# A fused attention and two-layer-pair kernel: low parts by products for unit 0 alone, two chunks loaded to other places, blocks alternating every two units

## The chip, the cores and the metric

The kernel runs on one core of a Trainium2 chip. The metric is the device time of one execution in microseconds. A core has a matrix engine (TensorE, PE in the profile, with its weight loads as PEld), VectorE (DVE), ScalarE (ACT), GpSimd (POOL) and SyncE (SP), which here issues all the transfers. Each engine takes its instructions strictly in program order.

## What is computed

Three stages on fp32 data, each feeding the next:

```python
# 1: decayed linear attention, batch 4, 8 heads, 768 steps, head size 48
state = alpha[:, :, t, :, None] * state + einsum('bhd,bhe->bhde', k[:, :, t], v[:, :, t])
y[:, :, t] = einsum('bhd,bhde->bhe', q[:, :, t], state)
# 2: x is y as 3072 tokens of 384; w_a, w_b 384 x 1536, w_out 1536 x 384
x = (x @ w_a) * (x @ w_b) @ w_out
# 3: w_in 384 x 2048, w_out 2048 x 384
h = x @ w_in
out = (maximum(h, 0) + alpha * minimum(h, 0)) @ w_out
```

The weights arrive as 64-bit floats, in halves that the kernel itself has to put together.

## The kernel before, in words

The 3072 tokens are six blocks of four chunks of 128 tokens. A block's four chunks (one for each batch entry) go through the attention, which leaves the block's x in `xt[n]`; then the block's 512 columns go through stage 2, and at the end all blocks go through stage 3.

**fp32 by three products.** PE multiplies values rounded to its fast format (fp32r). Every operand is therefore split into a high part h and a low part l, and a product is h*h + l*h + h*l (`mm3`, lines 601 to 604). One such product of 128x128 by 512 columns is three matmuls; a step of stage 2 (one half of a unit for one block) is 27 of them: nine into `pa`, nine into `pb`, nine into the three accumulators `acc`.

**Units.** Stage 2's hidden size 1536 is cut into six units of 256. Unit u has three weights, a, b and o, each 128 x 768. Each is loaded raw as 64-bit words and converted by `conv` (from line 224): ScalarE takes the magnitude into a tile c (line 253), DVE takes the sign (256), puts it in (261), keeps the power of two (265) and forms what fp32 leaves over (270), ScalarE rounds to the high part (276). Then comes the low part, x - high + rest. There are two ways: with `on_pe` false, two DVE operations (`sub`, line 279, `low`, line 282); with `on_pe` true, three fp32 products with plus and minus the identity into a PSUM tile `cl` (lines 307 to 309), in two halves of 384 columns, each evacuated by ScalarE (312). `PE_UNITS = 3` sends the nine weights of units 0, 1 and 2 the second way. The weights a0 and b0 are converted in two halves throughout, and are loaded raw to the places of later weights (`w17`, `w16`).

**Segments.** `SEGMENTS` says in which order blocks meet units: (block, first unit, end). Blocks 0 and 1 alternate: block 0 with units 0 to 2, block 1 with units 0 to 2, then both with 3 to 5. After a segment the accumulators go to a partial sum `part`: the first segment of a block is copied by ScalarE (`evict1`), a later one is added by DVE, three operations of 512 columns.

**A chunk of attention** (`chunk(g)`). Loads: ra (decays, line 365), kq (369), v (373; in block 0 also vg). DVE: scan backwards (387), reciprocal (393), scan forwards (397), scale k and q (402). PE: transpose k (`kps`, 440), scores (`A`, 457), state update (`dS`, 481), output (`y`, from 491). DVE masks the two score tiles (`As`, 464). ScalarE and DVE split y into the high (564) and low (568) part of x. Tiles ra, kq and v have two buffers each (`tp`), so chunk 2 waits for chunk 0's; `Ring` objects hold these waits.

**The order of work** is written by a planner. `Graph` collects operations with an engine, an assumed duration, a due key and their dependencies; `run` plays them through as a list schedule and emits each engine's instructions in the order that results. Where it sees PE idle for over 500 ns, `fill` (line 177 and on) emits dummy bf16 products `wp` for seven tenths of the hole, one per 110 ns.

Of the kernel before, what the change touches and what calls it, by code (L numbers as in the profile page):

```python
# [11 lines left out]
F32 = mybir.dt.float32  # L12
# [9 lines left out]
P = 128  # L22
CH = 128
# [1 line left out]
MB = BC * CH  # L25

SEGMENTS = (
    (0, 0, 3), (1, 0, 3), (0, 3, 6), (1, 3, 6),
    (2, 0, 6), (3, 0, 6), (4, 0, 6), (5, 0, 6),
)  # L30
LAG = 2

PE_UNITS = 3


MM = 228
# [102 lines left out]
def body(tc, akq, v, vg, w_a, w_b, w_o1, w_in, w_o2, beta, out):  # L139
# [3 lines left out]
    NU1, NU2 = w_a.shape[0], w_in.shape[0]  # L143
    F1, F2 = 2 * NU1, 2 * NU2
    UC = w_a.shape[2]
    NJ = H // 2
    D = KT * P // H
    GR = 64 - D
    NA = NJ * (CH + 1) + 1
# [3 lines left out]
    with ExitStack() as ctx:  # L153
        ctx.enter_context(tc.manual_schedule())
        pool = lambda name, bufs=1, **k: ctx.enter_context(tc.tile_pool(name=name, bufs=bufs, **k))
        const, wpool, pers = pool("const"), pool("wpool"), pool("pers")
        xpool, cpool, gpool, tp = pool("xpool", 2), pool("cpool", 2), pool("gpool", 2), pool("tp", 2)
# [50 lines left out]
        G = Graph(fill)  # L208
# [3 lines left out]
        flat = [(n, i, s) for s, (n, u0, u1) in enumerate(SEGMENTS) for i in range(2 * u0, 2 * u1)]  # L212
# [10 lines left out]
        def conv(src, tag, name, key, wait, sink, early=15000, on_pe=False, halves=None):  # L223
# [14 lines left out]
            for n in range(2 if halves else 1):  # L238
# [61 lines left out]
                for h in range(2 // N):  # L300
                    cut = lambda x, h=h: x[:, :, h * UC // 2 : (h + 1) * UC // 2] if N == 1 else x
                    p = {}

                    def add(p=p, cut=cut, c1=c1, c2=c2, hi=hi):
                        t = ps_mm.tile([P, MB], F32, name="cl", tag="mm")
                        o = p["t"] = t[:, 0 : UC // 2].rearrange("p (t f) -> p t f", t=nt)
                        nc.tensor.matmul(o, ident, cut(c1()), start=True, stop=False)  # L307
                        nc.tensor.matmul(o, minus, cut(hi()), start=False, stop=False)
                        nc.tensor.matmul(o, ident, cut(c2()), start=False, stop=True)

                    def low_pe(p=p, cut=cut, lo=lo):
                        nc.scalar.copy(cut(lo()), p["t"])
                        sink(b["r"])

                    y = G.add("PE", 900, add, key, [x], pool=mpool)
                    cring.use(y)
                    ev = G.add("ACT", 500, low_pe, key, [y], after=[ev])
                    y.hold.append(ev)
# [3 lines left out]
        def as_unit(r, n):  # L322
            return tuple(y.rearrange("p (t f) -> p t f", t=n) for y in (r[:, 0:UC], r[:, UC : 2 * UC]))

        done, slot_of, taken = {}, {}, {}
        for u in range(NU1):
            for nm, src in (("a", w_a), ("b", w_b), ("o", w_o1)):
                x = nm, u
                slot_of[x] = len(slot_of)
                uses[x] = []  # L330

                def sink(r, x=x):
                    units[x] = as_unit(r, 2 if x[0] == "o" else KT)


                spare = {("a", 0): 3 * NU1 - 1, ("b", 0): 3 * NU1 - 2}.get(x)
                ld, done[x] = conv(src[u], f"w{slot_of[x]}", f"{nm}{u}", due[x] - 20000,
                                   taken.pop(slot_of[x], ()), sink, on_pe=u < PE_UNITS,
                                   halves=None if spare is None else (f"w{spare}", KT))
                if spare is not None:  # L340
                    taken[spare] = done[x]

# [9 lines left out]
        def chunk(g):  # L352
# [6 lines left out]
            def A(eng, dur, fn, deps, early=0, lat=0, after=()):  # L359
                return G.add(eng, dur, fn, key - early, deps, lat, after)  # L360


            def load_a():
                s["ra"] = tp.tile([P, 2 * NA - 1], F32, name="ra", tag="ra")
                nc.sync.dma_start(s["ra"][:, NA - 1 :], akq[g, :, 0:NA])

            def load_kq():
                s["kq"] = tp.tile([P, 2, NJ, CH], F32, name="kq", tag="kq")
                nc.sync.dma_start(s["kq"].rearrange("p s j t -> p (s j t)"), akq[g, :, NA:])

            def load_v():
# [6 lines left out]
            kT = lambda: s["kq"][:, 0]  # L378
            qT = lambda: s["kq"][:, 1]
            r0 = lambda: s["ra"][:, 0 : NA - 1].rearrange("p (j t) -> p j t", j=NJ)[:, :, 0:1]  # L380
            la = A("SP", 800, load_a, rring.take(), 14000, 2500)
            lq = A("SP", 1500, load_kq, lring.take(), 13800, 2500, [la])
            lv = A("SP", 1000, load_v, vring.take(), 12000, 2500)


# [20 lines left out]
            sa = before["scan"] = A("DVE", 1250, scan_a, [rc])  # L406
            slack = SLACK if not start else 0
            k1 = q1 = A("DVE", 1220, mul, [lq, sa], 0, slack)
            rring.use(k1)


            zs = None
            if not start:
                def decayed():
                    z = Z[:, c, :, :]
                    nc.vector.tensor_tensor(out=z, in0=z, in1=r0().to_broadcast([P, NJ, D]),
                                            op=ALU.mult)

                zs = A("DVE", 360, decayed, [r, *state[c]])
                rring.use(zs)  # L420

            def ps_tile(nm, bank=None):
                if start and bank is not None:
# [12 lines left out]
            if not end:  # L436
                def pe_k():
                    s["kps"] = ps_tile("kps", 0)
                    for j in range(NJ):
                        nc.tensor.transpose(s["kps"][:, j, :], kT()[:, j, :], ident)  # L440

                def ev_k():
                    s["ks"] = tp.tile([P, NJ, P], F32, name="ks", tag="ks", bufs=1)
                    nc.scalar.copy(s["ks"], s["kps"])

                w, hold = bank(0)
                x = A("PE", 480, pe_k, [k1, *w])
                ks = A("ACT", 600, ev_k, [x, *kring.take()])
                hold.append(ks)
                lring.use(x)  # L450

            def pe_a():
                s["A"] = [ps_tile(f"A{i}", i + 1) for i in range(2)]
# [21 lines left out]
            if ks is not None:  # L475
                def pe_d():
                    s["dS"] = ps_att.tile([P, NJ, D], F32, name="dS", tag="att")
                    for j in range(NJ):
                        for i in range(2):
                            hs = slice(64 * i, 64 * i + 64)  # L480
                            nc.tensor.matmul(s["dS"][hs, j, :], s["ks"][:, j, hs],
                                             s["v"][:, 2 * j + i, 0:D], start=True, stop=True)

                ds = A("PE", 500, pe_d, [ks, lv, *aring.take()])
                dhold = aring.last()
                kring.use(ds)
                vring.use(ds)
# [29 lines left out]
                for j in range(NJ):  # L517
                    inter(j, j == NJ - 1)

            py = A("PE", 1350 if start else 500 if moved else 1600, pe_y, [a0, a1, lv, q1, zs, *aring.take()])  # L520
            yhold = aring.last()
            if moved:
                def ev_3():
                    s["y3"] = shift[:, KT, :]
                    nc.scalar.copy(s["y3"], s["y"][:, KT, :])

                def pe_m():
                    for j in range(KT):
                        intra(j, j == 0, False)
                    for j in range(KT):  # L530
                        inter(j, False)
                    for j in range(KT):
                        nc.tensor.matmul(s["y"][:, j, :], shift[:, j, :], s["y3"], start=False,
                                         stop=j == KT - 1)

                x = A("ACT", 280, ev_3, [py, *yring.take()])
                py = A("PE", 1900, pe_m, [x])
                yring.use(py)
            lring.use(pa, py)


            if not end:
# [173 lines left out]
        for k, (n, i, s) in enumerate(flat):  # L716
            u, o = divmod(i, 2)
            x = lambda n=n: xt[n]
            b = {}
            pa, ma, ba = up(at[k], [done["a", u][o], *xdone[n]], x, ("a", u), o,  # L720
                            [d for j in range(k - 1) for d in done["o", flat[j][1] // 2]
                             if flat[j][1] // 2 < PE_UNITS and k < 12] + [up_before])
            pb, mb, bb = up(at[k] + 9 * MM, [done["b", u][o], *xdone[n]], x, ("b", u), o, [pa])
            up_before = pb
            xuse[n].extend((pa, pb))

            def copy_a(b=b, ba=ba):
                b["a"] = gpool.tile([P, MB], F32, name="a_sb", tag="a_sb")
                nc.scalar.copy(b["a"], ba["t"])  # L729

            def mul(b=b, bb=bb):
                nc.vector.tensor_tensor(out=b["a"], in0=b["a"], in1=bb["t"], op=ALU.mult)  # L732

            ca = G.add("ACT", 590, copy_a, at[k] - URGENT, [pa, *bring.take()])
            ml = G.add("DVE", 690, mul, at[k] - URGENT, [ca, pb])
            ma.append(ca)
            mb.append(ml)
            glo[k] = gsplit((1, k), at[k] - URGENT, [ml], lambda b=b: b["a"])
            ghold[k] = gring.last()
            bring.use(glo[k])  # L740
            if k >= LAG:
                down1(k - LAG)
# [171 lines left out]
```

## Time and profile before

| | |
|---|---|
| device time, median of 3 runs | 1001.33 us (1000.56 to 1001.47) |
| the profiled execution | 1001.07 us |
| its span, first to last instruction | 999.4 us |
| PE busy | 985.8 us, 99% |
| PE's weight loads busy | 794.2 us, 79% |
| DVE busy | 594.8 us, 60% |
| ACT busy | 256.8 us, 26% |
| read and written in HBM | 74.8 MB and 26.7 MB |

Busy times count an instruction from its start to its end. Matmuls overlap, so a matmul's own duration is longer than the distance to the next one's start; where PE is full, the distance between starts is what an instruction costs. DVE's instructions overlap a little too. Idle time of an engine that is not the bottleneck costs nothing.

### The profile page before, as it was taken

Reading aid. Unit: us, or ns where it says so; the run is one execution under the profiler, and the core shown is the slowest. Engines: PE = TensorE matmul, PEld = TensorE weight load, DVE = VectorE, ACT = ScalarE, POOL = GpSimd, SP = SyncE. Lnnn points to the kernel's source line nnn. Section 1 sums busy time; section 2 is a strip of 40 time slices with the busy share of each in tenths; the row PEclk is TensorE's granted clock in tenths of the full one; section 3 lists DMA queues with packets and bytes.
Section 4 is the critical chain, followed back from the end, with each engine's and each line's share of the span. In section 5 each row is a group of like instructions: output and inputs, shape, how many; then the busy total and the mean of one; then the engine's idle time right before and its main releaser. Section 6 shows DMA issues by size and latency. Waiting matters only on the chain.

```text
span 999.4 us, 12894 instructions
## 1 busy us (share of the span) xinstructions
PE 985.8 (99%) x5364; PEld 794.2 (79%) x5364; DVE 594.8 (60%) x860; ACT 256.8 (26%) x421; POOL 5.5 (1%) x18
## 2 busy tenths in 40 slices
PE   6999999999999999999999999999999999999998
PEld 5776788877888888788778888888888888888886
DVE  7877798258768876884432225554554555545543
ACT  2444443232333333332122112111121111111111
POOL 2000000000000000000000000000000000000000
PEclk9999999999999999999999999999999999999999
DMA  9941200044544744551226561020020100200000
GB/s 364 362 181 53 65 12 11 1 169 117 185 155 152 252 185 147 209 195 55 64 79 221 190 221 64 1 95 1 1 95 1 64 31 1 95 1 1 32 0 32
DMA packets 30922, 103.92 MB, mean 104 GB/s; under 512 B 3472, under 2 KB 3984, under 8 KB 30864
## 3 DMA queue, kind: packets, MB, share of 16 engines
q1 hardware_dynamic: 30864, 103.11, 29.3%
q8 instruction: 42, 0.69, 0.3%
q14 instruction: 16, 0.13, 0.0%
HBM read 74.78 MB, written 26.74 MB: 102 GB/s over the span
## 4 chain that ended last, share of the span: by engine, by line
PE 99%; DVE 0%; DMA 0%; ACT 0%; issue 0%; DVEq 0%; ACTq 0%
PE acc L601 12%; PE acc L604 12%; PE acc L602 12%; PE pi L601 7%; PE pi L602 7%; PE pi L604 7%; PE pb L601 5%; PE pa L601 5%; PE pa L602 5%; PE pa L604 5%; PE pb L602 5%; PE pb L604 5%; PE A L457 3%; PE y L491 2%; PE y L497 2%; PE cl L307 1%
## 5 line engine op out<-in xcount | busy, mean ns | idle before, releaser
L624 ACT CAST gh<-ng 128x512 fp32r<-128x512 f32 x96 | 59.6, 621 | 327.6 <-DVE ng L828 275.0
L824 DVE TENSOR_SCALAR ng<-pi,betaT 128x512 f32<-128x512 f32 x96 | 72.1, 751 | 106.7 <-PE pi L604 105.8
L732 DVE TENSOR_TENSOR a_sb<-a_sb,pb 128x512 f32<-128x512 f32 x72 | 49.5, 687 | 113.8 <-PE pb L604 111.7
L628 DVE TENSOR_TENSOR gl<-ng,gh 128x512 fp32r<-128x512 f32 x96 | 66.4, 691 | 79.8 <-ACT gh L624 79.8
L601 PE MATMUL pi<-x,v 128*128 128x512 f32 x288 | 113.3, 393 | 0.0
L602 PE MATMUL acc<-gh,v 128*128 128x512 f32 x288 | 112.9, 392 | 0.0
L604 PE MATMUL acc<-gl,v 128*128 128x512 f32 x288 | 112.8, 392 | 0.0
L602 PE MATMUL pi<-x,v 128*128 128x512 f32 x288 | 112.7, 391 | 0.0
L601 PE MATMUL acc<-gh,v 128*128 128x512 f32 x288 | 112.4, 390 | 0.0
L601 PE MATMUL pb<-x,wb 128*128 128x512 f32 x216 | 87.0, 403 | 0.0
L601 PE MATMUL pa<-x,wa 128*128 128x512 f32 x216 | 86.3, 399 | 0.0
L601 PE MATMUL acc<-gh,wo 128*128 128x512 f32 x216 | 85.8, 397 | 0.0
L604 PE MATMUL acc<-gl,wo 128*128 128x512 f32 x216 | 84.9, 393 | 0.0
L602 PE MATMUL acc<-gh,wo 128*128 128x512 f32 x216 | 84.7, 392 | 0.0
L602 PE MATMUL pa<-x,wa 128*128 128x512 f32 x216 | 84.6, 392 | 0.0
L602 PE MATMUL pb<-x,wb 128*128 128x512 f32 x216 | 84.6, 391 | 0.0
L604 PE MATMUL pi<-x,v 128*128 128x512 f32 x288 | 81.5, 391 | 0.0
L729 ACT COPY a_sb<-pa 128x512 f32<-128x512 f32 x72 | 42.3, 587 | 151.3 <-PE pa L604 151.3
L624 ACT CAST gh<-a_sb 128x512 fp32r<-128x512 f32 x72 | 44.7, 621 | 132.8 <-DVE a_sb L732 132.8
L828 DVE SCALAR_TENSOR_TENSOR ng<-pi,ng 128x512 f32<-128x512 f32 x96 | 66.4, 691 | 3.1
L601 PEld LDWEIGHTS pi<-x,v 128*128 128x128 f32 x288 | 54.1, 188 | 13.8 <-DVE ng L828 2.1
L601 PEld LDWEIGHTS acc<-gh,v 128*128 128x128 f32 x288 | 54.1, 188 | 12.1
(107 smaller groups left out, 1472.4 us busy)
## 6 DMA issues: line engine op xcount, KB each, us to landing
kq<-in_akq SPq DMA_DIRECT2D x24, 512.0 KB, 3.7
w2d<-ws SPq DMA_DIRECT2D x16, 768.0 KB, 3.4
v<-w2d SPq DMA_DIRECT2D x16, 768.0 KB, 5.5
x2d<-x SPq DMA_DIRECT2D x18, 512.0 KB, 3.4
x<-x2d SPq DMA_DIRECT2D x6, 1536.0 KB, 7.0
ra<-in_akq SPq DMA_DIRECT2D x24, 258.5 KB, 2.8
v<-in_v SPq DMA_DIRECT2D x24, 256.0 KB, 4.3
rs<-in_w_in SPq DMA_DIRECT2D x8, 768.0 KB, 4.6
```

Source lines behind the costliest of these rows:

```text
L457: nc.tensor.matmul(s["A"][i][:, j, :], kT()[ps, j, :], qT()[ps, j, :], start=True, stop=True)
L491: nc.tensor.matmul(s["y"][64 * i : 64 * i + 64, j, :], s["v"][:, 2 * j + i, :], s["As", i][:, j, :], start=first, stop=last)
L497: nc.tensor.matmul(s["y"][ps, j, :], Z[ps, c, j, :], qT()[ps, j, :], start=False, stop=last)
L601: nc.tensor.matmul(o, lh, rh, start=first and n == 0, stop=False)
L602: nc.tensor.matmul(o, ll, rh, start=False, stop=False)
L604: nc.tensor.matmul(o, lh, rl, start=False, stop=last and n == len(pairs) - 1)
L624: nc.scalar.copy(gq[idx][0], src())
L628: nc.vector.tensor_tensor(out=gl, in0=src(), in1=gh.bitcast(F32), op=ALU.subtract)
L729: nc.scalar.copy(b["a"], ba["t"])
L732: nc.vector.tensor_tensor(out=b["a"], in0=b["a"], in1=bb["t"], op=ALU.mult)
L824: nc.vector.tensor_scalar(out=b["n"], in0=bh["t"], scalar1=0.0, scalar2=betaT[:, i : i + 1], op0=ALU.min, op1=ALU.mult)
L828: nc.vector.scalar_tensor_tensor(out=b["n"], in0=bh["t"], scalar=0.0, in1=b["n"], op0=ALU.max, op1=ALU.add)
```

## The change

Three edits, with one set of retuned planner durations.

1. `ON_PE` takes the place of `PE_UNITS`: of the nine weights that form their low part by products into `cl`, a0, b0 and o0 are left. The six weights of units 1 and 2 take the DVE way. The first products of a block no longer wait in the plan for the o weights of such units.
2. Chunks 2 and 3 of block 0 load ra and kq to `w14`, `w15` and `w12`, `w13`, the places of o4, a5, a4 and b4, and not to the two rotating buffers. The loads of those weights wait for the chunks in turn. They leave the rings, so that later chunks wait for others.
3. Blocks 0 and 1 alternate after every two units and not after every three: six segments in place of four.

```diff
@@ -25,12 +25,12 @@
 MB = BC * CH
 
 SEGMENTS = (
-    (0, 0, 3), (1, 0, 3), (0, 3, 6), (1, 3, 6),
+    (0, 0, 2), (1, 0, 2), (0, 2, 4), (1, 2, 4), (0, 4, 6), (1, 4, 6),
     (2, 0, 6), (3, 0, 6), (4, 0, 6), (5, 0, 6),
 )
 LAG = 2
 
-PE_UNITS = 3
+ON_PE = (("a", 0), ("b", 0), ("o", 0))
 
 
 MM = 228
@@ -312,7 +312,7 @@
                         nc.scalar.copy(cut(lo()), p["t"])
                         sink(b["r"])
 
-                    y = G.add("PE", 900, add, key, [x], pool=mpool)
+                    y = G.add("PE", 1600, add, key, [x], pool=mpool)
                     cring.use(y)
                     ev = G.add("ACT", 500, low_pe, key, [y], after=[ev])
                     y.hold.append(ev)
@@ -322,7 +322,7 @@
         def as_unit(r, n):
             return tuple(y.rearrange("p (t f) -> p t f", t=n) for y in (r[:, 0:UC], r[:, UC : 2 * UC]))
 
-        done, slot_of, taken = {}, {}, {}
+        done, slot_of, taken, loads = {}, {}, {}, {}
         for u in range(NU1):
             for nm, src in (("a", w_a), ("b", w_b), ("o", w_o1)):
                 x = nm, u
@@ -335,8 +335,9 @@
 
                 spare = {("a", 0): 3 * NU1 - 1, ("b", 0): 3 * NU1 - 2}.get(x)
                 ld, done[x] = conv(src[u], f"w{slot_of[x]}", f"{nm}{u}", due[x] - 20000,
-                                   taken.pop(slot_of[x], ()), sink, on_pe=u < PE_UNITS,
+                                   taken.pop(slot_of[x], ()), sink, on_pe=x in ON_PE,
                                    halves=None if spare is None else (f"w{spare}", KT))
+                loads[slot_of[x]] = ld
                 if spare is not None:
                     taken[spare] = done[x]
 
@@ -360,12 +361,25 @@
                 return G.add(eng, dur, fn, key - early, deps, lat, after)
 
 
+            spare = 3 * NU1 - 4 - 2 * (c - 2) if start and c >= 2 else None
+            if spare is None:
+                rwait, lwait = rring.take(), lring.take()
+                rhold, lhold = rring.last(), lring.last()
+            else:
+                rwait, lwait, rhold, lhold = (), (), [], []
+
+            def in_tile(nm, shape, k):
+                if spare is None:
+                    return tp.tile(shape, F32, name=nm, tag=nm)
+                return wpool.tile(shape, F32, name=nm, tag=f"w{spare + k}")
+
+
             def load_a():
-                s["ra"] = tp.tile([P, 2 * NA - 1], F32, name="ra", tag="ra")
+                s["ra"] = in_tile("ra", [P, 2 * NA - 1], 0)
                 nc.sync.dma_start(s["ra"][:, NA - 1 :], akq[g, :, 0:NA])
 
             def load_kq():
-                s["kq"] = tp.tile([P, 2, NJ, CH], F32, name="kq", tag="kq")
+                s["kq"] = in_tile("kq", [P, 2, NJ, CH], 1)
                 nc.sync.dma_start(s["kq"].rearrange("p s j t -> p (s j t)"), akq[g, :, NA:])
 
             def load_v():
@@ -378,8 +392,8 @@
             kT = lambda: s["kq"][:, 0]
             qT = lambda: s["kq"][:, 1]
             r0 = lambda: s["ra"][:, 0 : NA - 1].rearrange("p (j t) -> p j t", j=NJ)[:, :, 0:1]
-            la = A("SP", 800, load_a, rring.take(), 14000, 2500)
-            lq = A("SP", 1500, load_kq, lring.take(), 13800, 2500, [la])
+            la = A("SP", 800, load_a, rwait, 14000, 2500)
+            lq = A("SP", 1500, load_kq, lwait, 13800, 2500, [la])
             lv = A("SP", 1000, load_v, vring.take(), 12000, 2500)
 
 
@@ -406,7 +420,7 @@
             sa = before["scan"] = A("DVE", 1250, scan_a, [rc])
             slack = SLACK if not start else 0
             k1 = q1 = A("DVE", 1220, mul, [lq, sa], 0, slack)
-            rring.use(k1)
+            rhold.append(k1)
 
 
             zs = None
@@ -417,7 +431,7 @@
                                             op=ALU.mult)
 
                 zs = A("DVE", 360, decayed, [r, *state[c]])
-                rring.use(zs)
+                rhold.append(zs)
 
             def ps_tile(nm, bank=None):
                 if start and bank is not None:
@@ -447,7 +461,7 @@
                 x = A("PE", 480, pe_k, [k1, *w])
                 ks = A("ACT", 600, ev_k, [x, *kring.take()])
                 hold.append(ks)
-                lring.use(x)
+                lhold.append(x)
 
             def pe_a():
                 s["A"] = [ps_tile(f"A{i}", i + 1) for i in range(2)]
@@ -481,7 +495,7 @@
                             nc.tensor.matmul(s["dS"][hs, j, :], s["ks"][:, j, hs],
                                              s["v"][:, 2 * j + i, 0:D], start=True, stop=True)
 
-                ds = A("PE", 500, pe_d, [ks, lv, *aring.take()])
+                ds = A("PE", 620, pe_d, [ks, lv, *aring.take()])
                 dhold = aring.last()
                 kring.use(ds)
                 vring.use(ds)
@@ -517,7 +531,7 @@
                 for j in range(NJ):
                     inter(j, j == NJ - 1)
 
-            py = A("PE", 1350 if start else 500 if moved else 1600, pe_y, [a0, a1, lv, q1, zs, *aring.take()])
+            py = A("PE", 1600 if start else 600 if moved else 1600, pe_y, [a0, a1, lv, q1, zs, *aring.take()])
             yhold = aring.last()
             if moved:
                 def ev_3():
@@ -534,9 +548,14 @@
                                          stop=j == KT - 1)
 
                 x = A("ACT", 280, ev_3, [py, *yring.take()])
-                py = A("PE", 1900, pe_m, [x])
+                py = A("PE", 2200, pe_m, [x])
                 yring.use(py)
-            lring.use(pa, py)
+            lhold.extend((pa, py))
+            if spare is not None:
+                for k, ops in ((spare, rhold), (spare + 1, lhold)):
+                    for o in ops:
+                        o.users.append(loads[k])
+                        loads[k].need += 1
 
 
             if not end:
@@ -718,8 +737,7 @@
             x = lambda n=n: xt[n]
             b = {}
             pa, ma, ba = up(at[k], [done["a", u][o], *xdone[n]], x, ("a", u), o,
-                            [d for j in range(k - 1) for d in done["o", flat[j][1] // 2]
-                             if flat[j][1] // 2 < PE_UNITS and k < 12] + [up_before])
+                            [up_before])
             pb, mb, bb = up(at[k] + 9 * MM, [done["b", u][o], *xdone[n]], x, ("b", u), o, [pa])
             up_before = pb
             xuse[n].extend((pa, pb))
```

What it does to the order, at three places. On PE, behind the last product into pb of unit 1's first half (weight wb_663 before, the tile of b1): before, the products of o1's low part follow.

```order
L604 MATMUL pb<-x,wb_663 128x512 x3
L307 MATMUL cl<-c_697,plus 128x384
L308 MATMUL cl<-wo_781,minus 128x384
L309 MATMUL cl<-c_698,plus 128x384
L601 MATMUL acc_650<-gh,wo_551 128x512
```

After, at the same unit (its a is wa_677, its b wb_773), nothing of the kind stands between the products; attention does.

```order
L623 MATMUL pa<-x,wa_677 128x512 x3
L505 MATMUL y<-As_814,v 64x128
L505 MATMUL y<-As_837,v 64x128
L511 MATMUL y<-kq,Z 48x128 x2
L620 MATMUL pb<-x,wb_773 128x512
L621 MATMUL pb<-x,wb_773 128x512
```

What moved: the cl rows of units 1 and 2 are gone from PE (54 rows of cl before, 18 after). In their place, at four points between the first product of block 0 and the first of block 1, stand dummy products, as here the last of seven ahead of unit 1's first pb:

```order
L184 LDWEIGHTS ones
L184 MATMUL wp<-ones 128x256
L620 MATMUL pb<-x,wb_773 128x512
L621 MATMUL pb<-x,wb_773 128x512
```

The dummies are 58 in all before, all ahead of the first pa; after, they are 74: 41 ahead of the first pa and 33 (7, 4, 8 and 14) between it and block 1's first pa.

On DVE, at the conversion of a1 (work tiles c_557 and c_558 before):

```order
L261 SCALAR_TENSOR_TENSOR c_557<-c_557,c_558 128x768
L256 TENSOR_SCALAR c_597<-rb_301 128x768
L265 TENSOR_SCALAR c_558<-c_557 128x768
L261 SCALAR_TENSOR_TENSOR c_596<-c_596,c_597 128x768
L270 SCALAR_TENSOR_TENSOR c_558<-ra_233,c_558 128x768
L265 TENSOR_SCALAR c_597<-c_596 128x768
L464 TENSOR_TENSOR As_645<-A_606,mask 128x512
L270 SCALAR_TENSOR_TENSOR c_597<-rb_301,c_597 128x768
```

After (work tiles c_577 and c_578, weight tile wa_677), the subtraction and the low part stand behind it, between a step's own two operations:

```order
L270 SCALAR_TENSOR_TENSOR c_578<-ra_276,c_578 128x768
L478 TENSOR_TENSOR As_675<-A_646,mask 128x512
L478 TENSOR_TENSOR As_685<-A_647,mask 128x512
L750 TENSOR_TENSOR a_sb<-a_sb,pb 128x512
L279 TENSOR_TENSOR c_577<-c_577,wa_677 128x768
L407 RECIPROCAL invs<-ra 128x4
L647 TENSOR_TENSOR gl<-a_sb,gh 128x512
L282 TENSOR_TENSOR wa_677<-c_577,c_578 128x768
```

What moved: two more DVE rows for each of six weights. On SP's queue at the start, before, the first inputs of chunk 2 stand behind two weights:

```order
L373 DMA v<-in_v 128x512
L376 DMA vg<-in_vg 128x384
L373 DMA v<-in_v 128x512
L376 DMA vg<-in_vg 128x384
L233 DMA ra_158<-in_w_a 128x768
L233 DMA rb_161<-in_w_b 128x768
L365 DMA ra<-in_akq 128x517
L233 DMA ro_194<-in_w_o 128x768
```

After, chunks 2 and 3 come first:

```order
L379 DMA ra<-in_akq 128x517
L383 DMA kq<-in_akq 128x1024
L387 DMA v<-in_v 128x512
L390 DMA vg<-in_vg 128x384
L379 DMA ra<-in_akq 128x517
L383 DMA kq<-in_akq 128x1024
L233 DMA ra_196<-in_w_a 128x768
L233 DMA rb_228<-in_w_b 128x768
```

What moved: ra and kq of chunks 2 and 3 ahead of all weights (rows 7, 8, 11 and 12 of the queue, where ra stood at 11 and 13 and kq at 15 and 19).

## Rows read from the trace of the kernel before

**Rows 1.** The page's first part: busy us, share of the span, instructions.

```profile
PE 985.8 (99%) x5364; PEld 794.2 (79%) x5364; DVE 594.8 (60%) x860; ACT 256.8 (26%) x421; POOL 5.5 (1%) x18
```

**Rows 2.** The page's second part: tenths in 40 slices; PE, DVE, granted clock.

```profile
PE   6999999999999999999999999999999999999998
...
DVE  7877798258768876884432225554554555545543
...
PEclk9999999999999999999999999999999999999999
```

**Rows 3.** The waits of PE: who, for whom, us in total, times, longest.

```profile
PE kps L440 <- DVE invs L393: 8.7, 1, 8.7
```

**Rows 4.** Timeline of PE around 38 us: start, length, engine, line, operation.

```profile
36.72 1.70 PE L184 MATMUL wp<-ones 128*128 128x256 bf16 x14
38.18 0.48 PE L601 MATMUL pa<-x,wa 128*128 128x512 f32 x1
```

**Rows 5.** Timeline of PE from 42.4 to 47 us.

```profile
42.41 0.81 PE L307 MATMUL cl<-c,plus 128*128 128x384 f32 x2
...
43.87 0.86 PE L307 MATMUL cl<-c,plus 128*128 128x384 f32 x2
...
45.38 0.81 PE L307 MATMUL cl<-c,plus 128*128 128x384 f32 x2
...
46.85 0.60 PE L440 MATMUL kps<-plus,kq 128*128 128x128 f32 x4
```

**Rows 6.** The tile cl: count, ns (least, median, most), first and last start.

```profile
L308 PEld LDWEIGHTS cl<-wa,minus x6: 190/190/190, 26.0 to 78.8; 128*128 128x128 f32 x6
...
L312 ACT CAST wa<-cl x6: 479/480/487, 27.4 to 80.2; 128x384 fp32r<-128x384 f32 x6
```

**Rows 7.** Groups of DVE up to 140 us: busy us, mean ns, idle before.

```profile
L387 DVE TENSOR_TENSOR_SCAN ra<-ra,ones 128x516 f32<-128x516 f32 x9 | 11.0, 1223 | 5.0 <-DMA ra<-in_akq 5.0
L402 DVE TENSOR_TENSOR kq<-kq,ra 128x1024 f32<-128x1024 f32 x9 | 11.0, 1217 | 0.0
L464 DVE TENSOR_TENSOR As<-A,mask 128x512 f32<-128x512 f32 x16 | 10.6, 685 | 1.3 <-PE A L457 1.3
...
L732 DVE TENSOR_TENSOR a_sb<-a_sb,pb 128x512 f32<-128x512 f32 x10 | 6.9, 686 | 6.3 <-PE pb L604 5.3 <-ACT wb L276 1.0
...
L279 DVE TENSOR_TENSOR c<-c,wb 128x768 f32<-128x768 f32 x2 | 1.9, 954 | 0.4 <-ACT wb L276 0.4
```

**Rows 8.** Timeline of DVE from 47 to 50 us.

```profile
47.09 0.96 DVE L261 SCALAR_TENSOR_TENSOR c<-c,c 128x768 uint32<-128x768 uint32 x1
47.97 0.56 DVE L256 TENSOR_SCALAR c<-rb 128x768 uint32<-128x768 uint32 x1
48.44 0.55 DVE L265 TENSOR_SCALAR c<-c 128x768 uint32<-128x768 uint32 x1
```

**Rows 9.** Timeline of all engines up to 38 us.

```profile
3.56 1.23 DVE L387 TENSOR_TENSOR_SCAN ra<-ra,ones 128x516 f32<-128x516 f32 x1 [3.56 <-DMA ra<-in_akq]
...
9.70 2.08 PE L457 MATMUL A<-kq 48*128 48x128 f32 x16
...
14.68 1.23 DVE L387 TENSOR_TENSOR_SCAN ra<-ra,ones 128x516 f32<-128x516 f32 x1 [1.18 <-DMA ra<-in_akq]
...
16.96 1.16 PE L457 MATMUL A<-kq 48*128 48x128 f32 x16
...
37.35 0.56 DVE L568 TENSOR_TENSOR x<-y,x 128x384 fp32r<-128x384 f32 x1 [1.42 <-ACT x L564]
```

**Rows 10.** Work by stretch: its length, then PE, PEld, DVE, ACT, POOL, clock, DMA, GB/s.

```profile
0.00:25.00 25.00, 16.32 (x171) 13.71 (x173) 18.07 (x25) 6.23 (x13) 5.47 (x18) 1.00 0.95 364
...
38.00:60.00 22.00, 22.00 (x121) 15.88 (x120) 20.04 (x30) 9.92 (x17) 0.00 (x0) 1.00 0.93 347
```

**Rows 11.** Timeline of PE at block 1's first product.

```profile
120.41 0.39 PE L604 MATMUL acc<-gl,wo 128*128 128x512 f32 x1
120.64 0.39 PE L601 MATMUL pa<-x,wa 128*128 128x512 f32 x1
```

## The prediction

> **What bounds the kernel now.** I read the page's busy shares first [rows 1]: the matrix engine (PE) is busy 99% of a span of 999.4 us, VectorE (DVE) 60%, ScalarE 26%. The slices say where the rest lies [rows 2]: only the first shows PE below nine tenths, and DVE is fullest there and just behind it, 7 to 8 tenths over the first seven slices. The list of waits, asked for PE alone, has one line, 8.7 us at the very start [rows 3]. The timeline then splits the run in two. Up to 38.18 us PE works on block 0's four attention chunks, with dummy products (wp) in the holes; at 38.18 the first product with a weight begins [rows 4]. From there PE has no wait of its own, so the time that is left, 999.4 - 38.2 = 961.2 us, is PE's queue, the stores at its end included. Work taken out of that queue shortens the run one for one, unless the engine that takes it over leaves PE without input.
>
> **The work that leaves PE.** A group of low parts is three fp32 products into a tile cl. Three groups in a row start at 42.41, 43.87 and 45.38, and the next work starts at 46.85 [rows 5]: 4.44 / 3 = 1.48 us each; I use 1.49, since the other bursts run a little longer. Products overlap, so the step between starts is the cost and not the durations in the rows. There are 18 groups now (six records of line 308 for each of a, b and o, of which [rows 6] shows the a's); the order shows 6 after, those of a0, b0 and o0. So 12 x 1.49 = 17.9 us leave PE, and with them 12 of ScalarE's evacuations of 0.48 us [rows 6]. That the change doesn't do this can be left out: the order has 54 rows of cl before and 18 after. Before the first product with a weight three groups run now and two after it; behind it 15 now and 4 then. What leaves the dense part is therefore 11 x 1.49 = 16.4 us.
>
> The Trainium skill (Perfetto Trace Analysis, Identifying the Most-Contended Engine) speaks against reading so much from PE's busy share: it holds matmul occupancy to be a bad measure, since matmuls overlap, and takes the weight loads' busy share instead, which is 79% here [rows 1]. If weight loads alone set the pace, the 11 groups would be worth five loads each, 11 x 5 x 0.19 = 10.5 us instead of 16.4, by the loads' own duration [rows 6]. The trace speaks for the steps: the starts lie 1.48 us apart although five loads take 0.95.
>
> **What DVE takes over.** Six weights (a, b and o of units 1 and 2) now get a subtraction and an addition over 768 columns, 0.95 us each [rows 7]. In a dense stretch DVE's starts lie some 0.08 us closer than that: 47.09, 47.97, 48.44 [rows 8] give 0.87 us for a 0.95 us operation and 0.47 for one of 0.55. So 12 x 0.87 = 10.4 us are added. The two further segments add six additions of an accumulator to its partial sum, priced by the a*b product of the same shape (0.69 us [rows 7], step 0.60): 3.6 us, well behind block 1's start, each set between the last product of a segment and the next use of the accumulators, 18 products later (18 x 0.23 = 4.1 us of PE, by the step from 120.41 to 120.64 [rows 11]). There DVE has 1.2 us of steady work per step (27 products, 6.2 us) and a unit's conversion of 13.3 us every two to six steps; I take these six at nothing. Were that cover gone, they would cost at most their 3.6 us.
>
> **The start, up to the first product with a weight.** It needs all four chunks of block 0. Now, chunk 2's first input waits for chunk 0's buffer, and DVE waits 1.18 us for it at 14.68; at 37.35 DVE waits 1.42 us for ScalarE ahead of block 0's last low part [rows 9]. After, chunks 2 and 3 load to places of their own, and all are issued ahead of the weights. In the order DVE has up to block 0's last low part 5 + 5 scans at 1.14, 5 products kq at 1.13, 8 masks at 0.60 (all [rows 7], less 0.08), 4 low parts at 0.47 (0.56 at 37.35) and some 4 us of half conversions and reciprocals: 27.7 us. Begun at 3.56 [rows 9] that ends at 31.3 at the earliest. What remains as a wait is, first, the first mask: the cold products that feed it run to 11.7 in any case [rows 9], about 1 us; and second, block 1's first scan, which stands ahead of block 0's last masks on DVE and whose input is number 22 on SP's queue. By the mean rate of the first 25 us, 364 GB/s [rows 10], the 9.2 MB up to it have landed at 25.3, about a microsecond after DVE could take it (20.9 us of work stand ahead, begun at 3.56). So 33.4 us as estimate, bounds 31.6 (DVE never waits, plus the hop to PE) and 38.2 (no gain, as DVE's 27.9 us of the same stretch take 34.3 now).
>
> **From there to block 1.** Now this stretch is 38.18 to 120.64 [rows 4, 11], 82.5 us. Taking out 15 groups (22.4) and the two steps of unit 2, which segments of two units do not need yet (2 x 6.2), and putting back four groups (6.0), PE has 53.7 us of work: block 1 could start at 33.4 + 53.7 = 87.1. DVE's sum up to block 1's last low part is 17 scans (19.4), 8 products kq (9.0), 16 masks (9.6), 8 low parts (3.8), state updates and reciprocals (3.0, an estimate by their width), 8 operations of the units (4.8) and conversions (22.2, and 6.3 for the four halves of a0 and b0): 78.1, so 81.7 at the earliest. Five microseconds separate the two engines, so PE will wait here and there for DVE. The order marks where: 33 dummy products stand in this stretch after (none now), each laid where the plan has PE wait. They take 33 x 0.104 = 3.4 us by their own rate (14 in 1.46 us, from 36.72 to 38.18 [rows 4]), and the holes for which they are cut to seven tenths would be 33 x 0.11 / 0.7 = 5.2. Bounds: 3.4, since they run whether needed or not, and 8.5, if DVE keeps only the 81% density of its first stretch (50.4 / 0.81 - 53.7). I take 5.0, nearest to the plan's holes, and between what the first stretch and the next one say of DVE (busy 20.0 of 22 us from 38 to 60 [rows 10]).
>
> **Behind that.** In the order no dummy product stands there, PE's work is the same in another sequence, and unit 3 is needed 6 steps after block 1's start, 37 us, in which DVE has some 20 us to convert for it. SP's queue is held up by block 1's third kq load (it waits for the first chunk's products), with four weights of units 4 and 5 behind it; those are wanted some 70 us later. So the gain stays.
>
> **Sum.** 33.4 + 961.2 - 16.4 + 5.0 = 983.2 us of span, against 999.4. The profiled execution took 1.67 us more than its span (1001.07), which makes 984.9; the median of the runs lies 0.3 above that execution. I predict 985.0.
>
> **Rivals.**
> *DVE takes more back.* If DVE keeps its density of 81% behind 38 us too, and the start gains nothing, the two bounds together give 38.2 + 944.8 + 8.5 + 1.7 = 993. For it: DVE runs in order, and the masks of block 1 now stand behind conversions. Against it: the early loads take its largest wait away.
> *PE waits less.* DVE's floor in the start and only the dummies' own 3.4 us: 31.6 + 944.8 + 3.4 + 1.7 = 981.5, and some 2 us less if the products next to a burst of cl step closer too (an estimate, 0.2 us for each of 11): 979.5.
> *Weight loads are the pace.* 985 + 5.9 = 991.
> *Slower than now.* The first products run at half rate: 16 of line 457 take 2.08 us at 9.70 and 1.16 at 16.96 [rows 9], which is PE's lower clock level, 1.2 against 2.4 GHz. If the new holes between 33 and 92 us put PE back there, each microsecond of its work costs 0.79 more. It decides from 16.4 / 0.79 = 21 us of work on; with half of the stretch's 54 us it is a loss of 21, so about 1006. Against it: the granted clock is full in every slice [rows 2] (the record begins behind the slow first products), and the dummies fill the holes.
>
> **Chances.** 985 (978 to 990): 0.70. 993: 0.15. 991: 0.04. Gain lost to a DVE wait until the total is within 0.2% of 1001: 0.03. Slower: 0.03. Below 979: 0.05. A difference of 0.2% (2 us) is about what a measurement here can tell from none. Faster 0.94, same 0.03, slower 0.03. The range 978 to 993 leaves out the slower and equal cases and the part of the first rival above its sum.
>
> **What would show it.** Right: 18 cl records of line 308's kind become 6; the first pa starts at 31.6 to 35; block 1's first pa at 89 to 95; no PE wait behind. Wrong: a first pa at 37 or later says that DVE or the loads, not chunk 2's buffer, set the start; block 1 later than 97 says that DVE is the bound of the stretch; a granted clock below full in the third or fourth slice is the slower rival; and a PE wait behind 100 us means that a converted weight or an accumulator comes late.

## The result, and the profile after

The changed kernel takes 986.67 us (median of 4 runs, 985.53 to 986.97) against 1001.4 us for the kernel before: a ratio of 0.9851, with a 95% interval of 0.9839 to 0.9864. The prediction was 985.0, in a range of 978 to 993. The profiled execution took 986.91 us, its span 985.2 us.

The page's first two parts, of the kernel after, against [rows 1] and [rows 2]:

```profile
PE 970.0 (98%) x5320; PEld 784.1 (80%) x5320; DVE 607.1 (62%) x878; ACT 252.8 (26%) x409; POOL 4.4 (0%) x18
...
PE   6999999999999999999999999999999999999998
...
DVE  7898988577767887884332245554555555545553
...
PEclk9999999999999999999999999999999999999999
```

PE is still full from the second slice on, at full clock, with 15.8 us less to do; DVE has 12.3 us more: 8.4 of them lie in the first seven slices (149.9 us busy against 141.5), which now read 7 to 9. PE's list of waits after, against [rows 3] (us in total, times, longest), has two short lines more, both of waits ahead of the first product with a weight (28.96 to 33 us):

```profile
PE kps L454 <- DVE invs L407: 8.8, 1, 8.8
PE y L505 <- DVE As L478: 0.9, 2, 0.8
PE dS L495 <- DMA v<-in_v: 0.6, 1, 0.6
```

The low parts by products are 6 groups in place of 18: line 308 has two records for each name, where [rows 6] had six.

```profile
L308 PE MATMUL cl<-wa,minus x2: 632/632/633, 30.0 to 41.0; 128*128 128x384 f32 x2
...
L308 PE MATMUL cl<-wb,minus x2: 631/632/632, 34.9 to 43.2; 128*128 128x384 f32 x2
...
L308 PE MATMUL cl<-wo,minus x2: 630/631/632, 56.7 to 58.1; 128*128 128x384 f32 x2
```

The two places that split the run, from PE's timeline (start, length, engine, line, operation): the first product with a weight, at 36.73 (before 38.18, [rows 4]), and block 1's first, at 93.98 (before 120.64, [rows 11], with two steps more ahead of it).

```profile
36.73 0.50 PE L620 MATMUL pa<-x,wa 128*128 128x512 f32 x1
...
92.53 1.69 PE L184 MATMUL wp<-ones 128*128 128x256 bf16 x14
93.98 0.47 PE L620 MATMUL pa<-x,wa 128*128 128x512 f32 x1
```

| stretch | predicted | measured |
|---|---|---|
| start to the first pa | 33.4 us | 36.7 us |
| first pa to block 1's first | 53.7 of work + 5.0 of waits = 58.7 | 57.25, so 3.5 of waits and dummies if the work is 53.7 |
| block 1's first to the end of the span | 944.8 - 53.7 = 891.1 | 985.2 - 93.98 = 891.2 |

So the total is right to 0.2%, and the parts are right behind the first pa. The start was forecast 3.3 us too early, and the waits after it 1.5 us too long; that these two errors cancel in part is luck.

### The profile page after: what moved, and what is told of

Same layout as the page of the kernel before. It is cut to its first block, busy times and chain, and to the rows that moved or that the text cites. A ratio compares the mean times of both kernels' runs of the same rounds, so it can differ in the third digit from the quotient of the medians.

```text
span 985.2 us, 12798 instructions
## 1 busy us (share of the span) xinstructions
PE 970.0 (98%) x5320; PEld 784.1 (80%) x5320; DVE 607.1 (62%) x878; ACT 252.8 (26%) x409; POOL 4.4 (0%) x18
## 4 chain that ended last, share of the span: by engine, by line
PE 97%; DMA 1%; DVE 1%; ACT 0%; issue 0%; DVEq 0%; ACTq 0%
PE acc L620 12%; PE acc L623 12%; PE acc L621 12%; PE pi L620 7%; PE pi L621 7%; PE pi L623 7%; PE pb L620 5%; PE pa L620 5%; PE pa L623 5%; PE pb L621 5%; PE pa L621 5%; PE pb L623 5%; PE A L471 2%; PE y L505 2%; PE y L511 2%; PE dS L495 1%
```

## The experiments

The runs were made in three groups, in which the kernel before took 1000.79, 1000.78 and 1000.98 us. The second group has the changed kernel once more, 986.46 us (986.05 to 987.53); the runs with v in places of its own, without late dummies and with o0 on DVE stand beside it. The others are set against the same 986.46 across groups. All runs that start from the changed kernel keep its retuned planner durations; no run takes these alone.

**The changed kernel again.**

> The changed kernel once more, beside the next ones on the same chip: 985.5 to 987 us, first pa at 36.7.

986.46 us, with the first pa at 36.5 and block 1's first at 93.8. The profile repeats itself to 0.2 us.

### What each edit is worth

**The first edit alone, on the kernel before.**

```diff
-PE_UNITS = 3
+ON_PE = (("a", 0), ("b", 0), ("o", 0))
...
-                   ... on_pe=u < PE_UNITS,
+                   ... on_pe=x in ON_PE,
...
```

> The kernel before with the first edit alone: a0, b0 and o0 form their low parts by products, the six weights of units 1 and 2 on DVE; rings and segments of three units as before. Theory (the products that leave PE are only worth what DVE can keep up with, and the other two edits make the room): the order has 106 dummies behind the first pa, whose holes would be 106 x 0.11 / 0.7 = 16.7 us, so nearly all of the 16.4 us come back as waits: 994 to 1001 us, first pa at about 38 us. Rival (the gain is the products' own time, whatever the segments are): 984 to 987 us.

994.23 us (993.77 to 994.45), a ratio of 0.993. The 16 us of products are gone as they are in the changed kernel, but only 6.6 us arrive. PE is still full by its busy share; what fills it is dummies, 106 of them behind the first pa, which take 11.0 us at 0.104 each. Three of the holes near block 1's start, in PE's timeline of this kernel:

```profile
91.33 1.04 PE L184 MATMUL wp<-ones 128*128 128x256 bf16 x8
...
93.99 2.90 PE L184 MATMUL wp<-ones 128*128 128x256 bf16 x25
...
111.43 2.02 PE L184 MATMUL wp<-ones 128*128 128x256 bf16 x17
113.21 0.48 PE L601 MATMUL pa<-x,wa 128*128 128x512 f32 x1
```

Block 1's first product comes at 113.21, only 7.4 us ahead of the kernel before, although 16.4 us of products less stand in front of it. The rival, that the products' own time is the gain whatever the segments are, falls. How much of the dummies' 11.0 us PE would have had to wait in any case, no run of this kernel shows.

**The first edit undone in the changed kernel.**

```diff
-ON_PE = (("a", 0), ("b", 0), ("o", 0))
+ON_PE = tuple((nm, u) for u in range(3) for nm in "abo")
...
-                            [up_before])
+                            [d for j in range(k - 1) for d in done["o", flat[j][1] // 2]
+                             if flat[j][1] // 2 < 3 and k < 12] + [up_before])
```

> The changed kernel with the first edit undone: all nine weights of units 0 to 2 by products again, chunks 2 and 3 in places of their own, segments of two units. Theory: 12 groups of 1.49 us come back to PE, 17.9 us, and the 3.5 us of waits and dummies between the first pa and block 1 go (no dummy stands there in the order): 986.7 + 17.9 - 3.5 = 1001 us, with the first pa at 36.7. Rival (the loads and the segments bring a good part by themselves): 996 us or less.

1001.44 us, a ratio to the kernel before of 0.9999 (0.9989 to 1.0008). Edits 2 and 3, with the retuned durations, bring nothing without the first. The difference to the changed kernel is 15.0 us. In the two traces, the time from the first pa (here at 37.03) to the end of the span is 962.9 us against 948.5, 14.4 more; all 12 groups stand there. With the 3.4 us of 33 dummies that the changed kernel has behind the first pa and this one has not, the groups cost PE 17.8 us, 1.49 each.

**The second edit undone.**

```diff
-            spare = 3 * NU1 - 4 - 2 * (c - 2) if start and c >= 2 else None
+            spare = None
```

> The changed kernel with the second edit undone: chunks 2 and 3 wait for the two rotating buffers again. Theory (the edit brings what the first pa moved, 38.2 to 36.7, since DVE stops waiting for chunk 2): first pa at 38 to 39, 988 to 990 us. Rival 1 (the transfers are full in the first 35 us anyway, so the order of the loads moves nothing): 986.7. Rival 2 (my prediction's size of it, 4.7 us): 991.

985.64 us (985.42 to 986.61), 0.8 us below the changed kernel's median; the first four runs of the changed kernel (985.53 to 986.97) reach as low. So with segments of two units the second edit is worth nothing. The first pa is at 36.49, as with it. DVE's timeline of this kernel shows the old wait for chunk 2 back in its place, and no wait at block 1's first scan (the third row):

```profile
14.79 1.23 DVE L401 TENSOR_TENSOR_SCAN ra<-ra,ones 128x516 f32<-128x516 f32 x1 [1.17 <-DMA ra<-in_akq]
...
20.89 1.21 DVE L401 TENSOR_TENSOR_SCAN ra<-ra,ones 128x516 f32<-128x516 f32 x1
...
27.92 1.22 DVE L401 TENSOR_TENSOR_SCAN ra<-ra,ones 128x516 f32<-128x516 f32 x1
```

In the changed kernel it is the other way round: no wait for chunk 2, and 2.46 us at block 1's first scan, which comes at 30.05.

```profile
30.05 1.23 DVE L401 TENSOR_TENSOR_SCAN ra<-ra,ones 128x516 f32<-128x516 f32 x1 [2.46 <-DMA ra<-in_akq]
```

My account of the start, that chunk 2's buffer alone sets it, falls; and the early loads are not free, for they moved the wait.

**The third edit undone.**

```diff
-    (0, 0, 2), (1, 0, 2), (0, 2, 4), (1, 2, 4), (0, 4, 6), (1, 4, 6),
+    (0, 0, 3), (1, 0, 3), (0, 3, 6), (1, 3, 6),
```

> The changed kernel with the third edit undone: blocks 0 and 1 alternate after three units. Theory (two units for each block leave DVE the time for the converted low parts): 96 dummies stand behind the first pa in the order, 15 us of holes against 5, so some 8 to 11 us are lost: 994 to 998 us, first pa at 36.7 as before. Rival (the segments only cost six additions, their order gives nothing): 986 us.

994.34 us (994.18 to 996.8), 7.9 us slower than the changed kernel and the same as the first edit alone. The first pa comes earlier here, at 34.15: block 1's first scan now stands behind block 0's last low part in DVE's timeline.

```profile
33.50 0.56 DVE L587 TENSOR_TENSOR x<-y,x 128x384 fp32r<-128x384 f32 x1 [0.46 <-ACT x L583]
...
35.89 1.23 DVE L401 TENSOR_TENSOR_SCAN ra<-ra,ones 128x516 f32<-128x516 f32 x1 [1.50 <-DMA ra<-in_akq]
```

Yet block 1's first product comes at 111.96. Taking off the two steps more that stand ahead of it (2 x 6.2) leaves 99.6, against 94.0. The stretch from the first pa to block 1's, here and then in the changed kernel (length, PE, PEld, DVE, ACT, POOL, clock, DMA share, GB/s), shows which engine has more to do:

```profile
34.15:111.96 77.81, 77.22 (x576) 59.05 (x575) 71.33 (x107) 33.31 (x54) 0.00 (x0) 1.00 0.45 168
...
36.73:93.98 57.25, 57.25 (x460) 43.05 (x458) 51.60 (x81) 24.45 (x42) 0.00 (x0) 1.00 0.57 214
```

With segments of three, 96 dummies stand in the stretch, 10.0 us at 0.104 each; without them PE's own work is some 67 us, and DVE, with 71.3, has more. With segments of two PE has 53.8 and DVE 51.6. So the shorter segments are what lets DVE keep up: unit 2's three weights, 13.3 us of DVE, are due behind block 1's start and not in front of it. Some 4 of the 7.9 us lie in DVE's work by this count; how the rest divides between DVE's waits and the dummies' own time is not shown, for this kernel was not run without them.

This kernel and the first edit alone differ by the second edit and the retuned durations. Between them the first pa moves from 37.25 to 34.15, near the 33.4 that was forecast, and the total does not move (994.23 and 994.34). So the second edit may well bring the first pa forward where block 1's first scan is not in the way; whether the places do it or the new order on DVE is not shown.

### Why the first pa came late

SP's timeline of the changed kernel shows what stood in front of block 1's first input:

```profile
9.24 0.34 SPq L233 DMA_DIRECT2D rb<-in_w_b  x1
16.11 0.33 SPq L387 DMA_DIRECT2D v<-in_v  x1
...
18.08 0.43 SPq L233 DMA_DIRECT2D rb<-in_w_b  x1
21.26 0.33 SPq L387 DMA_DIRECT2D v<-in_v  x1
21.91 0.33 SPq L390 DMA_DIRECT2D vg<-in_vg  x1
22.34 0.42 SPq L379 DMA_DIRECT2D ra<-in_akq  x1
```

SP issues b0's load at 9.24 and nothing more until 16.11, since chunk 2's v still has only the two rotating buffers and waits for chunk 0's output (6.2 us); at chunk 3's v it stands once more, for 2.7 us. Behind them stand weights that wait for nothing. The stretches of 2.5 us (length, PE, PEld, DVE, ACT, POOL, clock, DMA share, GB/s) show the transfers falling from 427 GB/s to 233 in the meantime, in the changed kernel:

```profile
12.50:15.00 2.50, 2.50 (x18) 1.59 (x16) 2.50 (x5) 0.32 (x1) 0.00 (x0) 1.00 1.04 427
15.00:17.50 2.50, 2.50 (x33) 2.07 (x34) 1.97 (x3) 0.58 (x2) 0.00 (x0) 1.00 0.78 287
17.50:20.00 2.50, 2.50 (x42) 2.21 (x41) 1.91 (x4) 1.44 (x4) 0.00 (x0) 1.00 0.88 233
20.00:22.50 2.50, 2.50 (x34) 1.94 (x33) 2.50 (x5) 0.75 (x2) 0.00 (x0) 1.00 0.91 320
```

**v and vg of chunks 2 and 3 to places of their own** (those of o3 and b3), with the same waits handed to those weights' loads:

```diff
+            vslot = 3 * NU1 - 7 - (c - 2) if spare is not None else None
...
+                if spare is not None:
+                    both = wpool.tile([P, (H + 2 * KT) * 64], F32, name="v", tag=f"w{vslot}")
...
```

> The changed kernel with v and vg of chunks 2 and 3 loaded to places of later weights too (those of o3 and b3), so that SP's queue no longer stands for chunk 0's and 1's outputs. Theory (the first pa came 3.3 us later than predicted because SP stood 6.2 us at chunk 2's v while the transfers ran dry, and block 1's first input landed at 30.0 in place of 25.3, with DVE waiting 2.5 us): that input lands by 26 to 28, DVE's wait for it falls under 1 us, first pa at 34.4 to 35.3, total 1.4 to 2.5 us less than the changed kernel beside it. Rival (the transfers are full, and more of them early only makes a0's weights late; or DVE's waits for PE's scores set the start): first pa at 36.5 or later, total the same within 0.7 us.

985.3 us (985.23 to 985.44), 1.2 us below the changed kernel beside it, a little under the 1.4 that I gave as the least. The transfers no longer run dry:

```profile
15.00:17.50 2.50, 2.50 (x32) 1.88 (x29) 2.26 (x3) 0.27 (x1) 0.00 (x0) 1.00 1.06 416
17.50:20.00 2.50, 2.50 (x41) 2.10 (x40) 1.67 (x3) 1.29 (x4) 0.00 (x0) 1.00 1.02 420
20.00:22.50 2.50, 2.50 (x35) 2.06 (x33) 2.50 (x5) 0.40 (x2) 0.00 (x0) 1.00 1.03 417
```

DVE's timeline of this kernel has block 1's first scan at 27.97 with no wait at all, and the first pa is at 35.13:

```profile
27.50 0.55 DVE L261 SCALAR_TENSOR_TENSOR c<-c,c 128x384 uint32<-128x384 uint32 x1
27.97 1.22 DVE L414 TENSOR_TENSOR_SCAN ra<-ra,ones 128x516 f32<-128x516 f32 x1
```

The mechanism is as stated: the wait of 2.5 us is gone, 1.4 us of it arrives at the first pa. In this execution DVE's first scan starts 0.3 us later than in the changed kernel (3.94 in place of 3.67) and PE's first wait is 9.3 us in place of 8.8, which may take part of the rest.

### Whether PE or DVE sets the stretch up to block 1

**Without the dummies behind the first pa.**

```diff
-            if t is None or t > t0 + 100:
+            if t is None or t > t0 + 100 or begun:
```

`begun` is filled by the first product with a weight.

> The changed kernel without the 33 dummies behind the first pa. Theory A (they run whether needed or not, and PE's real waits there are short: 0.9 us in the list): block 1's first pa comes up to 3.4 us earlier, total 1.5 to 3.4 us less. Theory B (they lie wholly in waits for DVE): 0 within 0.5 us. Theory C (they hold PE's clock up): the granted clock drops somewhere between 37 and 94 us and the total rises by 1 us or more.

984.47 us (983.63 to 985.75), 2.0 us less than the changed kernel beside it; block 1's first product comes at 91.56 in place of 93.77. The granted clock is 1.000 over the span, so theory C falls. Of the 3.4 us of the 33 dummies, 2.2 were cost and 1.2 lay in real waits; the two waits behind the first pa in the list come to 1.0. PE's waits now stand in the list under their own names (the first line is the start's):

```profile
PE y L506 <- DVE As L479: 0.6, 2, 0.4
PE pa L621 <- ACT x L584: 0.6, 1, 0.6
PE y L506 <- ACT shift L540: 0.4, 1, 0.4
```

**o0's low part on DVE too.**

```diff
-ON_PE = (("a", 0), ("b", 0), ("o", 0))
+ON_PE = (("a", 0), ("b", 0))
```

> The changed kernel with o0's low part on DVE as well, so that only a0 and b0 go by products. Theory (PE and DVE are near balance in the stretch from the first pa to block 1: PE loses 2 x 1.49 = 3.0 us of work, DVE gets 1.74 more): the order has 78 dummies there in place of 33, 12.3 us of holes against 5.2, so it ends 2 to 5 us later: 988 to 991. Rival (PE is still the bound there): 3 us less, 983.7.

987.87 us (987.57 to 988.66), 1.4 us more than the changed kernel beside it: the right sign, a smaller size than the 2 to 5 I gave. Taking 3.0 us from PE lengthens the run, so PE no longer is the bound of this stretch by itself.

**Both gains together, and the same with o0 on DVE.**

> The changed kernel with v and vg of chunks 2 and 3 in places of their own and without the dummies behind the first pa. Theory (the two gains lie in different stretches, 1.2 us ahead of the first pa and 2.0 us behind it, and add): 986.5 - 3.2 = 983.3 us, first pa at 35.1, block 1's first pa at 90.2. Rival (DVE is the bound up to block 1, so what one gives the other takes): 984.3 to 984.8, block 1 at 91.5.

982.33 us (982.26 to 982.91), a ratio to the kernel before of 0.9817 (0.9804 to 0.983), 4.1 us below the changed kernel. The first pa is at 34.44, block 1's first at 89.36. The two gains add, and 0.9 us more than their sum (1.2 and 2.0) comes out, 0.7 of it at the first pa (34.44 against 35.13 with v in its own places alone, where PE's first wait was 9.3 us; here it is 8.7). This is the best of all the kernels here.

> The same with o0's low part on DVE as well. Theory (o0 on DVE lost 1.4 us only because 78 dummies stood behind the first pa, 8 us of PE by their step, of which some ran longer than PE had to wait; PE's work is 3.0 us less): 1 to 2.5 us below the one beside it, 981 to 982.3. Rival (DVE, with 1.7 us more, sets the start of block 1): the same or up to 1.5 us slower than the one beside it.

983.58 us (983.29 to 984.12), 1.25 us slower than the one beside it. My theory, that the dummies alone had made o0's move a loss, falls: without a dummy behind the first pa the move costs the same. PE's waits of this kernel, without the start's:

```profile
PE y L519 <- ACT shift L553: 1.7, 3, 0.9
PE acc L639 <- DVE wo L283: 1.5, 1, 1.5
PE pa L638 <- ACT x L601: 0.6, 1, 0.6
```

The second line is new: a product into acc waits 1.5 us for line 283, which writes o0's low part on DVE. The first was 0.4 us, once, in the kernel beside it. From the first pa to block 1's PE waits 4.1 us here against 1.0 there, which takes back the 3.0 us of work. DVE is busy 51.5 of 55 us from 37 to 92 there, 50.4 in the kernel beside it:

```profile
37.00:92.00 55.00, 50.81 (x412) 38.10 (x410) 51.52 (x78) 23.50 (x39) 0.00 (x0) 1.00 0.56 213
```

## Why the prediction was right, and where not

**What leaves PE** (16.4 us behind the first pa, 17.9 in all): right. The first edit undone puts 17.8 us back, 1.49 us a group, as the steps gave. That settles the rival of the weight loads too: five loads of 0.19 us are 0.95 us a group, 11.4 us for the 12, and the run is 15.0 us longer. The Trainium skill (Perfetto Trace Analysis, Identifying the Most-Contended Engine) judges how close TensorE is to its limit by the rate of useful work (MFU) and the weight loads' busy share, and not by the matmuls' busy share. Taken as a price for removed work, which the page does not offer it as, the loads' time is too low in this case. Here the distance between starts, not the loads' busy share, told what the work was worth.

**The start** (33.4 us): the step that failed, by 3.3 us. I sized block 1's first input by bytes over the mean rate, as if SP's queue never stood. The text has chunks 2 and 3 loading to places of their own, but this holds for ra and kq alone: the queue stood 6.2 us at chunk 2's v and 2.7 at chunk 3's, the transfers fell to 233 GB/s, and DVE waited 2.5 us for that input in place of about one. Most of the rest of the miss is in DVE's waits for PE's scores and ScalarE's high parts (0.8, 0.6, 0.5 and 0.3 us after; I had counted about 1 us). What I gave as the reason for the gain here does not hold by itself: with the second edit undone the first pa is just as early, and with segments of two units the edit is worth nothing until v has its places too. The 1.5 us that the first pa did gain come with the other edits and the retuned durations; which part of them makes it I did not separate. The number that the text named as the sign of this error, a first pa at 37 or later, was nearly reached, and its sign of being right, 31.6 to 35, was missed.

**The stretch up to block 1** (53.7 us of work and 5.0 of waits): the work is right, the waits were 3.5, close to the lower bound of 3.4. Running without dummies shows that 1.2 us are waits in truth, so the plan's holes were too long, and the dummies, which I took for a bound, were two thirds cost. That PE and DVE are near balance there is right: less work for PE (o0 on DVE) costs 1.25 to 1.4 us.

**The six additions at no cost, and nothing behind block 1's start**: right. From block 1's first product on the run takes 891.2 us, where 891.1 were forecast, and PE's list of waits has no line on an accumulator.

**The two further edits.** The sum took all three together and did not say which one carries it. The runs do: the first edit alone brings 6.6 us; segments of two units, tried with the retuned durations, bring the rest; the places for chunks 2 and 3 bring nothing to the total, with segments of two or of three.

**The rivals.** DVE taking more back (993) is what happens with segments of three units (994.2 and 994.3); the segments are why it did not happen here. That PE waits less (981.5) fell with the start. The slower case fell: the granted clock stays full, with and without the dummies.

## What to carry to other kernels

Work taken off a full engine pays in full only where the engine that takes it over has slack at that moment: sum the second engine's work up to the same due point, and look for the edit that moves the due point (here two units in place of three were worth 8 us, dummies included). On an in-order issue queue the arrival of a transfer is not bytes over rate: look for the first entry that waits for compute, and for what stands behind it; giving a buffer to one of a chunk's loads and not to the others only moves the wait. Filler instructions laid by an assumed schedule are work too: their own time is lost where the real wait is shorter.

## What the runs showed that I had not expected

Without dummies behind the first pa, over a stretch in which PE waits six times for 0.3 to 1.5 us (o0 on DVE, v in its own places), the granted clock stayed at full. And one load can take far longer than the median of its kind: block 1's first input, issued at 22.34 behind a queue that was just filling again, was in use only at 30.05, 7.7 us later, with DVE waiting for it, where the page gives a median of 3.2 us. That the loads issued beside it are the reason is likely, and not shown.

```profile
ra<-in_akq SPq DMA_DIRECT2D x24, 258.5 KB, 3.2
```
